# Two kinds of attention, four layers, one core: which score banks VectorE exponentiates is chosen while the program is written out, not beforehand

## The chip, the cores and the metric

One core of a Trainium2 chip. The time is that of one execution on the device, in microseconds (us); three executions of the kernel before took 2189.13, 2195.17 and 2195.78, median 2195.17. Engines: PE (TensorE, matrix products), ACT (ScalarE, here the exponentials), DVE (VectorE), POOL (GpSimd) and SP, which starts most loads. Each works through its own list of instructions in order and waits for the others by semaphores.

## What is computed

Four residual layers over x of 2048 rows and 640 columns, bf16: layers 0 and 2 with attention in a window of 256 keys (weights A), layers 1 and 3 with full attention over all 2048 keys (weights B). 32 heads of 20 columns.

```python
def _B_ref(x, wqkv, wo):
    ...
    scores = jnp.einsum("bhqd,bhkd->bhqk", q, k) * (Dh ** -0.5)
    p = _softmax(scores, axis=-1)
    o = jnp.einsum("bhqk,bhkd->bhqd", p, v)
    return (lambda x, *d: x.transpose(*d))(o, 0, 2, 1, 3).reshape(B, S, D) @ wo
...
x = A_x
x = x + _A_ref(_layernorm(x, axis=-1), A_wqkv, A_wo)
x = x + _B_ref(_layernorm(x, axis=-1), B_wqkv, B_wo)
x = x + _A_ref(_layernorm(x, axis=-1), A_wqkv, A_wo)
x = x + _B_ref(_layernorm(x, axis=-1), B_wqkv, B_wo)
```

`_A_ref` is the same with scores masked to keys at most 255 rows back.

## The kernel before

**Units, banks, tiles.** Queries go in four chunks of 512 rows, heads in eight groups of four. A *unit* (l, c, g) is the attention of layer l, query chunk c, head group g. Chunk 0 of layers 1 and 3 is cut by keys too: (3,0,g,(0,12)) does key blocks 0 to 11 of 16, (3,0,g,(12,16)) the last four, which only become known when chunk 3 of layer 2 is done. A *bank* is one head's scores of 128 keys against 512 queries: one PSUM bank, [128, 512]. A unit of full attention has 64 banks. The list `units` (L750 to L766) fixes the order: layer 0 mixed with the first part of layer 1, then layer 1 with the windowed units of layer 2 between, then layer 3. The "second layer" is layer 1, the "final layer" layer 3.

The main loop (L1324) writes out one *tile* at a time, mostly three banks: score matmuls into one of two halves of PSUM (banks 0 to 2, or 3 to 5), one exponential on ACT over all of it (L1387), and two or three tiles later the products with the values into bank 7 (`op`, L1420). Where a tile has the first bank of a unit not yet met, `state["unit"]` is set to that unit and `start_unit` is called (L1338 to L1348). The order of PE's instructions is the order in which the loop and the functions it calls write them.

**Background.** All other work is in generators (`Task`): `t_ln` (normalise and transpose a chunk), `t_v` (values, eight blocks of a chunk), `t_block` (keys or queries, five blocks of 128 columns), `t_out` (output projection and residual), `t_tail` (division by the softmax sums). Keys, queries and values go through DRAM (`k_d`, `q_d`, `v_d`): stored by POOL, loaded for a unit by `load_unit` on SP. `background` calls `pump` once a tile with a credit from `rate`, which looks how much is left to do until the unit that needs it (`starts`, in tiles), and then `keep_clock`, which adds matmuls that nobody reads (`unread`, or `owed` ones in the next tile) until the tile has 1.76 groups of background matmuls. Every step takes a PSUM bank by `take_m`. Once the wide units begin (`end_early`), bank 6 alone is left for this. A tail goes ahead of all other tasks. `load_ahead` loads the next units as soon as all that they need is `ready`; if a unit starts and something is not ready, `start_unit` calls `require`, which writes out the missing tasks on the spot.

**Banks for DVE.** Some banks are exponentiated by DVE instead: `side_fixed` reads the scores into fixed point (L957), `t_chain` makes the exponential of a pair of banks in four operations (L969, L978, L980, L982), `side_values` multiplies with the values. Before, `put_aside` names them when the units are made: the last banks of each unit, four in layer 1 (`SIDE_1`), six or eight in layer 3 (`SIDE_3`), none in chunk 0 and in (3,1,0). In layer 1 the list `tiles` is laid out in advance, with such a bank as the third of every fifth tile, its scores in the tile's own half of PSUM. In layer 3, chunks 1 to 3, one is started (`side_scores`, into bank 6, which it keeps for two ticks) when `state["lag"]`, an estimate of DVE's backlog, is under `LAG`. The buffers for it in layer 3 are three tiles of the pool of transposed chunks (`side_start`); this waits until no transposed chunk is alive and nothing is left to do.

Of the kernel before, what the change touches and what calls it, by code (L numbers as in the profile page):

```python
# [23 lines left out]
NT = S // P  # L24
# [15 lines left out]
LAG = 0.5  # L40
WORK = 1.0
SIDE_1 = 4
SIDE_3 = (6, 8)
# [9 lines left out]
def kernel(  # L53
# [272 lines left out]
    def evac(out_, in_):  # L326
        if state["act"]:
            nc.scalar.copy(out=out_, in_=in_)
        else:
            state["lag"] += 0.6  # L330
            nc.vector.tensor_copy(out=out_, in_=in_)  # L331
# [60 lines left out]
    def stats(l, c, i):  # L392
        if (l, c) not in mvs:
            mvs[l, c] = lnp.tile([P, 4, 2], F32, name="mv", tag="mv")
        state["lag"] += 1.2
        st = lnp.tile([P, 2, 6], F32, name="stats", tag="stats")
        xv = x_sb[:, 4 * c + i, :]
        nc.vector.bn_stats(out=st[:, 0, :], in_=xv[:, 0:HD])
        nc.vector.bn_stats(out=st[:, 1, :], in_=xv[:, HD:D])
        nc.vector.bn_aggr(out=mvs[l, c][:, i, :], in_=st[:])  # L400
# [282 lines left out]
    def put_aside(l, c, g):  # L683

        if l == 1:
            n = SIDE_1
        else:
            n = 4 if (c, g) == (NC - 1, G - 1) else SIDE_3[g % 2]
        if n == 2:
            return ((NT - 1, 2), (NT - 1, 3))  # L690
        return tuple((NT - 1 - i // 4, i % 4) for i in range(n))

# [3 lines left out]
    class Unit:  # L696
        def __init__(self, l, c, g, part=None):
            self.l, self.c, self.g, self.part = l, c, g, part
            self.windowed = l % 2 == 0
            self.aside = ()  # L700
            if self.windowed:
                sets = [(m, b0, subs, j) for m, b0, subs in window_banks(c) for j in range(4)]
            else:

                if c > 0 and (l, c, g) != (3, 1, 0):
                    self.aside = put_aside(l, c, g)
                k0, k1 = key_blocks(l, part)
                sets = [
                    (None, 0, [(kc, 0, 4, 0)], j) for kc in range(k0, k1) for j in range(4)
                    if (kc, j) not in self.aside  # L710
                ]
            n = len(sets)
            self.banks = [
                (self, j, m, b0, subs, i < 4, i >= n - 4 + len(self.aside), i == n - 1)
                for i, (m, b0, subs, j) in enumerate(sets)
            ]
# [144 lines left out]
    def finish_unit(u):  # L861
# [31 lines left out]
    side_todo = deque(  # L893
        (u, p, i) for u in units for p in range(len(u.aside) // 2) for i in range(2)
    )
    side_left = Counter({id(u): len(u.aside) for u in units})
    side_out = {}
    side = {"xi": deque(), "chain": deque(), "out": deque(), "late": False}
# [7 lines left out]
    def side_start():  # L906

        assert live["xnT"] == 0 and not side["chain"] 
        tl = [xtp.tile([P, KD, C], BF16, name="xnT", tag="xnT") for _ in range(3)]
        live["xnT"] += 3  # L910
        f = [v[:, 0:4, :].rearrange("p a b -> p (a b)").bitcast(F32) for v in tl]
        side["xi"].clear()
        side["out"].clear()
        outs = [ka_all[:, KA - 6 + 2 * n : KA - 4 + 2 * n, :] for n in range(3)]
        outs += [qa_all[:, 2 * n : 2 * n + 2, :] for n in range(2)]
        side_tiles(f[0:2], f[2].bitcast(F16)[:, 0 : 2 * C], outs)
        side["late"] = True
# [9 lines left out]
    def side_free():  # L927

        if not side_todo or not side["late"]:
            return False  # L930
        u, p, i = side_todo[0]
        return (
            id(u) in loaded and state["tick"] >= loaded[id(u)] + 8
            and mfree[6][0] <= state["tick"] and (i == 1 or len(side["xi"]) > 0)
        )

    def side_scores():

        u, p, i = side_todo[0]
        mseq[0] += 1  # L940
        mfree[6] = (state["tick"] + 2, mseq[0])
        kc, j = u.aside[2 * p + i]
# [4 lines left out]
    def side_fixed(z):  # L947

        u, p, i = side_todo.popleft()
        side_left[id(u)] -= 1  # L950
        if not side_left[id(u)] and id(u) in deferred:
            live["kt"] -= 1
            live["qt"] -= 1
        if i == 0:
            side["now"] = side["xi"].popleft()
        xi = side["now"]
# [33 lines left out]
    def side_work(force):  # L990

        while (force or state["lag"] < WORK) and side["chain"]:
# [11 lines left out]
    def side_values(u, pairs, done):  # L1004

        for n in range(done, len(pairs)):
            pt = pairs[n][0]
            for i in range(2):
                kc, j = u.aside[2 * n + i]
                nc.tensor.matmul(  # L1010
                    op[32 * j : 32 * j + VW, :], lhsT=u.v(kc, j), rhs=pt[:, i, :], start=False,
                    stop=all(jj != j for _, jj in u.aside[2 * n + i + 1 :]),
                    skip_group_check=True,
                )
            side["out"].append(pt)

    def side_push():
# [3 lines left out]
        if side_free():  # L1021
            side_scores()
# [7 lines left out]
    def side_done(u):  # L1030

        n = 0
        while len(side_out.get(id(u), ())) < len(u.aside) // 2:
            n += 1
            assert n < 10000
            side_push()
        return side_out.pop(id(u))
# [5 lines left out]

    def s_emitted(u):
# [6 lines left out]
        elif side_left[id(u)]:  # L1051
# [187 lines left out]
    with tc.manual_schedule():  # L1239
# [11 lines left out]
        banks = [b for u in units for b in u.banks]  # L1251
        tiles = []
        starts = {}
        n = 0
        last_layer = sum(len(u.banks) for u in units[: index[3, 1, 0, None]])
        placed = {}
        while n < last_layer:
            size = 2 if len(tiles) % 2 and narrow(banks[n][0]) else 3
            u = banks[n][0]
            at = placed.setdefault(id(u), [])  # L1260
            extra = []
            if (
                len(at) < len(u.aside) and banks[n + 1][0] is u
                and len(tiles) >= (15 // (SIDE_1 - 1) if SIDE_1 > 2 else 3) * len(at) + (at or [0])[0]
            ):
                kc, j = u.aside[len(at)]
                extra = [(u, j, "side", 0, [(kc, 0, 4, 0)], False, False, False)]
                at.append(len(tiles))
                size = 2
            for b in banks[n : n + size]:  # L1270
                starts.setdefault(id(b[0]), len(tiles))
            tiles.append(banks[n : n + size] + extra)
            n += size
        for m, b in enumerate(banks[n:]):
            starts.setdefault(id(b[0]), len(tiles) + m // 3)
        banks = deque(banks[n:])

        side_now = False

        def next_tile(t):  # L1280

            if t < len(tiles):
                return tiles[t]
            size = 3
            if side_now:
                return [banks.popleft() for _ in range(min(size, len(banks)))]
            if t % 2 and not tails and state["held"] is None and mfree[6][0] < state["tick"]:
                if all(task.wake > state["tick"] for task in todo) :
                    size = 4
            return [banks.popleft() for _ in range(min(size, len(banks)))]  # L1290

        def rate(t):

            if t >= len(tiles):
                return 0.45
            u = tiles[t][0][0]
            if index[u.l, u.c, u.g, u.part] < woven:
                return 1.2
            done, r = 0.0, 0.6 if state["early"] else 0.3
            for task in todo:  # L1300
                done += max(task.left, 0.0)
                if task.need < len(units):
                    r = max(r, done / max(starts[id(units[task.need])] - t - 16, 1))
# [10 lines left out]
        last_tick[0] = len(tiles)  # L1314
# [4 lines left out]
        valued = 0  # L1319
# [4 lines left out]
        while ended is None or t < ended + 8:  # L1324
# [3 lines left out]
            if t < len(tiles) or banks:  # L1328
                if t >= len(tiles) and not side["late"] and not live["xnT"] and not todo:
                    side_start()  # L1330
                side_now = (
                    state["held"] is None and state["lag"] < LAG and side_free()
                )
                cur = next_tile(t)
# [28 lines left out]
                if cur[-1][2] == "side":  # L1363
                    cur = cur[:-1]
                    n_b -= 1
                    if "early" not in side:
                        side_early()
                    while not side_todo[0][2] and not side["xi"]:
                        assert side_work(True)
                    side_fixed(sp[:, n_b, :])  # L1370
                if side_now:
                    side_scores()
# [28 lines left out]
            for n in range(2 if n_b == 0 or t > closed + 1 else 0):  # L1401
# [15 lines left out]
                for m, (kc, q0, qn, col) in enumerate(subs):  # L1417
                    for _, pg, i, b in group:
# [4 lines left out]
                            start=(first and m == 0), stop=(last and m == len(subs) - 1),  # L1423
                            skip_group_check=u.windowed or len(u.aside) > 0,
                        )
                if first:
                    valued = 0
                if u.aside and not end:
                    pairs = side_out.get(id(u), ())
                    if len(pairs) > valued and pairs[valued][1] + 3 <= state["tick"]:  # L1430
                        if valued + 1 < len(u.aside) // 2:
                            side_values(u, pairs[: valued + 1], valued)
                            valued += 1
                if end and u.aside:
                    side_values(u, side_done(u), valued)
# [87 lines left out]
```

## Time and profile before

| | us |
|---|---|
| median of three executions | 2195.17 (2189.13 to 2195.78) |
| the profiled execution | 2197.81 |
| its span, first to last instruction | 2196.1 |
| mean granted clock of PE in it | 0.993 |

Where the span goes, from the starts of the exponentials in the timeline (the first tile of each stretch):

| stretch | from | to |
|---|---|---|
| layer 0, and with it the first parts of layer 1's chunk 0 | 16.4 | 441.2 |
| last part of layer 1's chunk 0 | 441.2 | 498.6 |
| layer 1, chunks 1 to 3, with layer 2, chunks 0 to 2 | 498.6 | 1285.6 |
| layer 3, chunk 0, key blocks 0 to 11, with layer 2, chunk 3 | 1285.6 | 1501.5 |
| layer 3, chunk 0, key blocks 12 to 15 | 1501.5 | 1559.8 |
| layer 3, chunks 1 to 3 | 1559.8 | 2183.5 |

How to read it: a row of a group is line, engine, operation, output and input with their shapes, count; then busy time and mean duration in ns; then the engine's idle time just before these instructions and who ended it. A row of the timeline is start, duration, engine, line, operation. Matmuls into four strips of 32 columns run side by side, four instructions make one *group* (L307, L1420).

### The profile page before, as it was taken

Reading aid. Unit: us, or ns where it says so; the run is one execution under the profiler, and the core shown is the slowest. Engines: PE = TensorE matmul, PEld = TensorE weight load, DVE = VectorE, ACT = ScalarE, POOL = GpSimd, SP = SyncE. Lnnn points to the kernel's source line nnn. Section 1 sums busy time; section 2 is a strip of 40 time slices with the busy share of each in tenths; the row PEclk is TensorE's granted clock in tenths of the full one; section 3 lists DMA queues with packets and bytes.
Section 4 is the critical chain, followed back from the end, with each engine's and each line's share of the span. In section 5 each row is a group of like instructions: output and inputs, shape, how many; then the busy total and the mean of one; then the engine's idle time right before and its main releaser. Section 6 shows DMA issues by size and latency. Waiting matters only on the chain. (4 is left out here: it accounts for less than half of the span.)

```text
span 2196.1 us, 73000 instructions
## 1 busy us (share of the span) xinstructions
PE 1931.1 (88%) x31782; PEld 760.4 (35%) x31783; DVE 1324.3 (60%) x2308; ACT 2112.9 (96%) x1726; POOL 483.3 (22%) x952
## 2 busy tenths in 40 slices
PE   8999998988889888888888988888888988888887
PEld 3444443433333333333333433342222222222222
DVE  5556565425656666566665743532487778778873
ACT  7789899999999999999999999999999999999997
POOL 6665556110121113401143112511000000000000
PEclk9899999999999999999999999999999999999999
DMA  6223233322210323112231123122112111111100
GB/s 201 74 82 107 68 98 99 81 78 64 74 46 27 83 60 90 39 37 64 64 101 34 35 86 98 39 57 65 48 43 61 32 32 41 35 32 35 53 20 17
DMA packets 88416, 137.27 MB, mean 63 GB/s; under 512 B 20766, under 2 KB 63486, under 8 KB 88094
## 3 DMA queue, kind: packets, MB, share of 16 engines
q1 hardware_dynamic: 68878, 79.43, 13.1%
q0 software_dynamic: 19216, 53.17, 8.2%
q8 instruction: 249, 4.08, 0.8%
q14 instruction: 73, 0.60, 0.1%
HBM read 99.52 MB, written 27.79 MB: 58 GB/s over the span
## 5 line engine op out<-in xcount | busy, mean ns | idle before, releaser
L1387 ACT ACTIVATE pt<-ps 128x1536 bf16<-128x1536 f32 (+2 forms) x1646 | 2072.1, 1438 | 46.1 <-PE ps L1359 36.1
L1359 PE MATMUL ps<-qt,kt 32*128 32x512 bf16 x3938 | 542.4, 384 | 79.3 <-ACT pt L1387 70.2
L307 PE MATMUL ps<-masks,ident 128*32 128x512 bf16 x5676 | 504.6, 387 | 99.4 <-ACT pt L1387 54.8
L1420 PE MATMUL ps<-pt,vt 128*21 128x512 bf16 x3826 | 383.1, 387 | 1.1 <-issue 1.1
L1359 PEld LDWEIGHTS <-kt 32*128 32x128 bf16 x3938 | 161.0, 91 | 482.7 <-issue 461.0
L307 PEld LDWEIGHTS <-ident 128*32 128x32 bf16 x5676 | 179.9, 94 | 283.1 <-issue 254.7
L1463 POOL TENSOR_SCALAR_AFFINE_SELECT pt<-pt 128x256 bf16<-128x256 bf16 (+2 forms) x505 | 213.2, 444 | 184.4 <-ACT pt L1387 181.8
L307 PE MATMUL ps<-xnT,wqk 128*32 128x512 bf16 x3320 | 224.8, 381 | 12.4 <-DVE on L1128 2.8
L331 DVE CAST st<-ps 128x512 bf16<-128x512 f32 x134 | 92.7, 691 | 169.1 <-PE ps L307 164.9
L1420 PEld LDWEIGHTS <-vt 128*21 128x21 bf16 x3842 | 95.0, 89 | 254.9 <-issue 251.5
L957 DVE TENSOR_SCALAR xnT<-ps 128x512 int32<-128x512 f32 x158 | 109.2, 691 | 109.2 <-PE ps L944 108.4
L307 PE MATMUL ps<-wop,on 128*32 128x320 bf16 x3712 | 160.9, 300 | 6.8 <-DVE x_sb L579 3.3
L1474 DVE TENSOR_TENSOR pt<-pt,masks 128x512 bf16<-128x512 bf16 (+4 forms) x267 | 111.3, 433 | 61.3 <-ACT pt L1387 59.8
L307 PEld LDWEIGHTS <-on 128*32 128x32 bf16 x5760 | 122.2, 95 | 66.6 <-issue 33.6
L1359 PE MATMUL ps<-qa,ka 32*128 32x384 bf16 (+2 forms) x1408 | 114.5, 278 | 24.4 <-ACT pt L1387 21.2
L307 PE MATMUL ps<-wv,xnT 128*32 128x320 bf16 x2560 | 116.6, 302 | 7.9 <-DVE on L1128 3.3
L579 DVE TENSOR_TENSOR x_sb<-x_sb,ps 128x320 bf16<-128x320 bf16 x120 | 58.3, 486 | 105.8 <-PE ps L307 104.9
L307 PEld LDWEIGHTS <-wqk 128*32 128x32 bf16 x3320 | 83.5, 96 | 95.9 <-issue 38.0
L1128 DVE TENSOR_TENSOR on<-on,ps 128x512 bf16<-128x512 bf16 x128 | 86.3, 683 | 47.8 <-PE ps L307 46.9
L885 DVE CAST on<-ps 128x512 bf16<-128x512 f32 x112 | 77.1, 688 | 61.7 <-PE ps L1010 36.1
L957 DVE TENSOR_SCALAR raw_o<-ps 128x512 int32<-128x512 f32 x96 | 66.1, 689 | 61.4 <-PE ps L1359 60.3
L546 POOL DMA_DIRECT2D k_d<-st x75 | 42.6, 568 | 224.2 <-DVE st L331 209.1
(101 smaller groups left out, 1638.5 us busy)
## 6 DMA issues: line engine op xcount, KB each, us to landing
vt<-v_d SPq DMA_DIRECT2D x48, 336.0 KB
kt<-k_d SPq DMA_DIRECT2D x192, 80.0 KB
wqk<-in_B_wqkv_dram POOLq DMA_DIRECT2D x80, 160.0 KB, 3.5
wqk<-in_A_wqkv_dram POOLq DMA_DIRECT2D x70, 160.0 KB, 3.5
k_d<-st POOLq DMA_DIRECT2D x75, 128.0 KB, 2.3
q_d<-st POOLq DMA_DIRECT2D x75, 128.0 KB, 2.1
qt<-q_d SPq DMA_DIRECT2D x384, 20.0 KB
v_d<-vs POOLq DMA_DIRECT2D x16, 336.0 KB, 3.1
```

The source lines that it names most:

```text
L307: nc.tensor.matmul(out_[r], lhsT=lhsT[:, r], rhs=rhs, start=start, stop=stop)
L331: nc.vector.tensor_copy(out=out_, in_=in_)
L546: nc.gpsimd.dma_start(out=dst, in_=staging.pop())
L579: nc.vector.tensor_tensor(out=xv, in0=had, in1=yp, op=ALU.add)
L885: nc.vector.tensor_copy(out=oT, in_=op)
L957: nc.vector.tensor_scalar(out=xi.bitcast(I32)[:, i * C : (i + 1) * C], in0=z, scalar1=SCALE * LOG2E * FIX, scalar2=127.5 * FIX, op0=ALU.mu ...
L1128: nc.vector.tensor_tensor(out=oT, in0=oT, in1=zb, op=ALU.mult)
L1359: nc.tensor.matmul(sp[:, i, col * P : (col + qn) * P], lhsT=u.k(kc, j), rhs=u.q(j, q0, qn), start=True, stop=True,)
L1387: nc.scalar.activation(out=pt[:, i:k, b0 * P :], in_=sp[:, i:k, b0 * P :], func=ACT.Exp, scale=SCALE,)
L1420: nc.tensor.matmul(op[32 * j : 32 * j + VW, q0 * P : (q0 + qn) * P], lhsT=u.v(kc, j), rhs=pg[:, i, col * P : (col + qn) * P], start=(first ...
L1463: nc.gpsimd.affine_select(out=v, in_=v, compare_op=ALU.is_gt if later else ALU.is_ge, fill=0.0, base=0, pattern=[[0, k - i], [-1 if later ...
L1474: nc.vector.tensor_tensor(out=pt_[:, i:k, cols], in0=pt_[:, i:k, cols], in1=mv_, op=ALU.mult)
```

## The change

Every unit now has a queue `rest` from which the loop takes its next banks one by one (`pop`), instead of a list made in advance; `put_aside` and the list `tiles` are gone. Before each tile the loop asks `side_giver` for a unit that can give a bank to DVE: only while the lag is under `LAG` (`LAG_1` before layer 3's buffers are there), from the current unit or one of the next two that has been loaded for eight ticks, as long as it has 30 banks left (`KEEP`; 12 once it has begun to give); in layer 1 at most four a unit (`MOST_1`), in layer 3 without a limit. `side_take` takes two from the queue's end. Layer 1's chunk 0 is left out, layer 3's chunk 0 is not: `side_start` now comes from unit (3,0,4) on, as soon as at most one transposed chunk is alive. `rate` reckons the position from `state["unit"]` and what is left in it. Some estimates of lag change.

```diff
+LAG_1 = 0.5
 WORK = 1.0
-SIDE_1 = 4
-SIDE_3 = (6, 8)
+WORK_1 = 1.0
+KEEP = 30
+MOST_1 = 4
 QA = 4
...
-            state["lag"] += 0.6
+            state["lag"] += 0.7 if in_.shape[-1] == C else 0.5
...
-                if c > 0 and (l, c, g) != (3, 1, 0):
-                    self.aside = put_aside(l, c, g)
-                k0, k1 = key_blocks(l, part)
...
+                self.k0, k1 = key_blocks(l, part)
+                self.rest = deque((kc, j) for kc in range(self.k0, k1) for j in range(4))
+            self.size = len(self.rest)
+
+        def pop(self):
+
+            if self.windowed:
+                return self.rest.popleft()
+            kc, j = self.rest.popleft()
+            end = not self.rest
+            return (self, j, None, 0, [(kc, 0, 4, 0)], kc == self.k0, end, end)
 
...
-        assert live["xnT"] == 0 and not side["chain"] 
+        assert live["xnT"] <= 2 and not side["chain"] and side["half"] is None
...
+    def side_giver():
+
+        if side["half"] is not None:
+            return side["half"][0]
+        if not side["xi"]:
+            return None
+        while side["at"] < len(givers) and not givers[side["at"]].rest:
+            side["at"] += 1
+        for n in range(side["at"], min(side["at"] + 3, len(givers))):
+            u = givers[n]
+            if id(u) not in loaded or state["tick"] < loaded[id(u)] + 8:
+                return None
+            if not side["late" if u.l == 3 else "early"]:
+                return None
+            if u.l == 1 and len(u.aside) >= MOST_1:
+                continue
+            if len(u.rest) >= (KEEP if len(u.rest) + len(u.aside) < u.size else 12):
+                side["at"] = n
+                return u
+        return None
+
+    def side_take(u):
+
+        if side["half"] is not None:
+            return side["half"][1]
+        j = u.rest.pop()
+        i = u.rest.pop()
+        u.aside += (i, j)
+        side["half"] = (u, i, j)
+        return i
...
+        starts, spans = {}, {}
+        n = 0.0
+        for u in units:
+            starts[id(u)] = n
+            spans[id(u)] = u.size / (2.5 if narrow(u) else 3.0)
+            n += spans[id(u)]
+        flow = deque(units)
...
+        def next_tile(t, giver):
+
+            if state["unit"] < final:
+                size = 2 if t % 2 and narrow(flow[0]) else 3
+                if giver is None or giver.l == 3 or size == 2:
+                    return take(size)
+                kc, j = side_take(giver)
+                return take(2) + [(giver, j, "side", 0, [(kc, 0, 4, 0)], False, False, False)]
...
-            if index[u.l, u.c, u.g, u.part] < woven:
+            u = units[state["unit"]]
+            if state["unit"] < woven:
                 return 1.2
+            now = starts[id(u)] + spans[id(u)] * (1 - len(u.rest) / u.size)
             done, r = 0.0, 0.6 if state["early"] else 0.3
             for task in todo:
                 done += max(task.left, 0.0)
                 if task.need < len(units):
-                    r = max(r, done / max(starts[id(units[task.need])] - t - 16, 1))
...
+                if not side["early"] and state["unit"] >= index[1, 1, 0, None]:
+                    side_early()
+                if (
+                    not side["late"] and state["unit"] >= index[3, 0, 4, PARTS[3][0]]
+                    and live["xnT"] <= 1 and not live["qa"] and not live["ka"]
+                ):
                     side_start()
-                side_now = (
-                    state["held"] is None and state["lag"] < LAG and side_free()
-                )
-                cur = next_tile(t)
+                if state["unit"] >= final:
+                    last_tick[0] = 0
+                giver = side_giver() if state["lag"] < (LAG if side["late"] else LAG_1) else None
+                if giver is not None and giver.l == 3 and (
+                    state["held"] is not None or mfree[6][0] > state["tick"]
+                ):
```

## The prediction

> **What bounds the kernel now.** First the shares of busy time, then ACT's groups by shape.
>
> ```profile
> PE 1931.1 (88%) x31782; PEld 760.4 (35%) x31783; DVE 1324.3 (60%) x2308; ACT 2112.9 (96%) x1726; POOL 483.3 (22%) x952
> ...
> L1387 ACT ACTIVATE pt<-ps 128x1536 bf16<-128x1536 f32 x1321 | 1816.3, 1549 | 37.0 <-PE ps L1359 28.4 <-POOL pt L1463 3.0 <-issue 1.7
> L1387 ACT ACTIVATE pt<-ps 128x1024 bf16<-128x1024 f32 x245 | 261.2, 1070 | 8.4 <-PE ps L1359 7.8
> L1387 ACT ACTIVATE pt<-ps 128x512 bf16<-128x512 f32 x21 | 13.3, 639 | 0.0
> ```
>
> ACT is nearly always busy, and with exponentials. Their ends overlap, so the price of a tile is read from starts, in the chain of waits:
>
> ```profile
> 1530.56 0.64 ACT pt L1387
> 1531.89 0.65 ACT pt L1387
> 1533.22 0.67 ACT pt L1387
> ```
>
> 1.33 us per 1536-column tile. From the starts of all exponentials in the timeline, 1024 columns take 0.90, 768 0.69, 512 0.48, 256 0.26. With these widths, all waiting of ACT from the start of unit (1,1,0) at 498.6 us to the end adds up to 47 us; 92 us lie before (layer 0 and its mixture with layer 1), where the change alters nothing but a few fillers. So behind 498 us a bank that leaves ACT is worth its full width, and whatever delays the next scores by more than about one tile is paid in full: the PSUM halves let PE be one tile ahead, no more.
>
> PE has little room. A tile's scores and its value matmuls begin 0.33 us apart each (timeline at 1440.75, 1441.07, 1441.41), a four-strip group of 512 columns adds 0.21 and one of 320 columns 0.13; `keep_clock` fills up to 1.76 groups a tile. A tile with eight groups of 320 needs 0.66 + 1.17 = 1.83 us, more than 1.33.
>
> **The change, part by part.** *Banks taken from ACT.* The instruction orders of both programs give the counts: layer 1 hands 96 banks to DVE in both (24 units, four each, so the cap of four changes nothing in number), layer 3 hands over 186 instead of 158. ACT's instructions go 1321 to 1316 (1536 columns), 245 to 238 (1024), 28 to 26 (768), 21 to 26 (512), 15 to 13 (256): 5 x 1.33 + 7 x 0.90 + 2 x 0.69 - 5 x 0.48 + 2 x 0.26 = 12.5 us less (14.7 by mean durations). Of the 28 banks 22 come from layer 3's chunk 0: ten pairs from units (3,0,4) to (3,0,7) and one from (3,0,4,(12,16)). The DVE work for them (14 chains of 0.69, 0.69, 1.22 and 1.22 us and 28 reads of 0.69, together 73 us) lies beside ACT, DVE being 60% busy. Cost of their reads on bank 6 by the row of units (3,1,0) to (3,1,7), which do the same now: 7.3 us of waiting in eight units against 0.8 in (3,0,4) to (3,0,7); four units: +2 (0 to 4).
>
> *What this moves.* Bank 6 is the only PSUM bank for background work by then, and each score on it blocks it for two ticks, each tail, `out` or projection step having to find it free. In the order of before, the last tail of layer 2 ends early in (3,0,4), `out(2,3)` follows, `ln(3,3)` and the values fill (3,0,5) and (3,0,6), and keys block 0 stands 17 tiles ahead of (3,0,0,(12,16)), the first unit that needs them. In the changed order the tails of layer 2 crawl through (3,0,4) and (3,0,5), `out(2,3)` gets one 320-column step of eight groups every fifth tile, its last four in consecutive tiles (4 x 0.5 over, less the one tile of lead: +1.5), and nothing of `ln(3,3)` but its rstd stands before the first tile of (3,0,0,(12,16)). There `start_unit` calls `require`, and on PE, ahead of that tile's scores, stand in one piece: four transposed rows of `ln(3,3)`, all eight value blocks, keys block 0; on SP behind it the loads of `vt`, `qt`, `kt`. The whole runs through bank 6 alone, PE and DVE in turn. The same pieces now, from the timeline:
>
> ```profile
> 1457.17 0.46 PE L447 MATMUL ps<-ident,xn 128*32 128x128 bf16 x20
> 1457.69 0.49 DVE L331 COPY xnT<-ps 128x640 bf16<-128x640 bf16 x1 [0.43 <-PE ps L447]
> 1461.09 0.86 PE L307 MATMUL ps<-wv,xnT 128*32 128x320 bf16 x20 [0.18 <-DVE xnT L331]
> 1462.00 0.49 DVE L331 CAST vs<-ps 128x320 bf16<-128x320 f32 x1 [0.96 <-PE ps L307]
> 1462.55 0.86 PE L307 MATMUL ps<-wv,xnT 128*32 128x320 bf16 x20
> 1479.87 1.25 PE L307 MATMUL ps<-xnT,wqk 128*32 128x512 bf16 x20
> 1481.18 0.69 DVE L331 CAST st<-ps 128x512 bf16<-128x512 f32 x1 [3.55 <-PE ps L307]
> ```
>
> A value block takes 1.46 us from start to start (0.91 until its eviction, 0.49, 0.06), eight 11.7. A transposed row takes 0.21 of fillers, 0.52 and 0.49 + 0.06: 1.28; four with the first without fillers 4.9. Keys 1.25 + 0.05 + 0.69 = 2.0. Then the round trip through DRAM:
>
> ```profile
> 1476.93 0.69 DVE L331 CAST st<-ps 128x512 bf16<-128x512 f32 x1 [2.54 <-PE ps L307]
> 1477.93 0.56 POOL L546 DMA_DIRECT2D k_d<-st  x1 [0.50 <-DVE st L331]
> 1480.72 0.28 SPq L812 DMA_DIRECT2D kt<-k_d  x1
> 1482.17 0.33 SPq L812 DMA_DIRECT2D kt<-k_d  x1
> 1556.50 2.03 DMA kt<-k_d
> ```
>
> Eviction done at 1477.62, first `kt` issue at 1480.72, the third strip, which the tile's third bank reads, 1.45 later, landed 2.03 later: 6.6 us. With 0.4 for scores and about 1.1 until the first normalised row is there (0.16 + 0.47 behind a 1.22 chain step), the chain is 1.1 + 4.9 + 11.7 + 2.0 + 6.6 + 0.4 = 26.7 us, counted from where these scores would have been issued; ACT has one tile left: 25.4 us of standstill. No other unit may run meanwhile, since ACT and PE go in order.
>
> PE's clock makes it longer:
>
> ```profile
> 50.10:53.50 3.40, 1.22 (x37) 1.00 0.74 190
> 53.00:56.00 3.00, 2.83 (x54) 1.46 (x58) 0.74 (x2) 1.78 (x3) 0.78 (x2) 0.59 0.32 82
> 1517.80:1521.25 3.45, 2.25 (x57) 1.00 0.34 99
> 1521.25:1524.70 3.45, 3.45 (x32) 0.51 0.06 17
> ```
>
> (PE's busy time, then the granted clock.) After 3.4 us with 2.25 us busy or less the clock was granted at half for 3.4 us. In the value chain PE is busy 0.86 of 1.46, 59%, in the rows of transposes less; at half clock a value block's PE part grows by about 0.65. Half of the blocks cold: 4 x 0.65, with rows and keys about +3.5 (0 to 7). I take 29 us for the standstill, 22 to 35.
>
> The Trainium skill, "TensorE: Matmul & The Clock Gate", Part 1, has the clock halve after an idle window of some 3.4 us. The trace's 2.25 of 3.45 us is not idle and was followed by half clock all the same. By the page's wording the 3.5 us would be nothing and the standstill 25.4; I go by the row.
>
> *Next late:* keys block 1, for (3,0,1,(12,16)), is put out behind the second tile after the standstill: 0.74 for the fourth strip, two 0.33 for values, 0.2 for the side values, 1.25 to 2.3 on PE (clock cold after 6.6 us of idling), 0.75, 3.1 to the first `kt`, 0.74 and 2.03 to the second strip, 0.4: 10 to 11 us, with five tiles, 6.7 us, to cover it: +4 (2 to 6). The remaining key and query blocks have unloaded PE then and are hidden by that wait.
>
> *Layer 1.* The banks go as lag allows, also from units one or two ahead, and that marks such a unit as started: `state["unit"]` jumps ahead and then stays there while earlier units still run, so `rate` is first high, later low. Projection groups per tile: 2.5 or more in 8 of 24 units before (1.5 us of waiting each in the trace; the other 16 have 0.8 each), in 13 units in the changed order, six of them at 3.0 to 3.3; the fillers of layers 1 and 2 grow by 71 groups where the work is missing. 5 x 0.7 = 3.4 at least by the class means, 9 if those above 3 wait twice that: +5 (-2 to 10, since the spread within a class is as large as the step).
>
> Sum: -12.5 + 2 + 1.5 + 29 + 4 + 5 = +29. The profiled execution took 2197.8 (span 2196.1 and 1.7 around it), so 2226.8; it lies 2.6 above the median of 2195.2, so 2224 for a median.
>
> **Rivals.** *The chain is shorter.* PE alone would need 8 x 0.86 + 4 x 0.45 + 1.25 = 9.9 us; if evictions hid and the clock held, with 7.0 for the round trip and 1.1 at the front, 18 - 1.3 = 16.7: sum +14 with layer 1 at +3, 2209. For it: DVE is idle then. Against: one bank, and 1462.55 follows 1462.49. Chance 0.15.
>
> *Everything is cold.* Half clock through all the chain and on through the blocks behind it, standstill 35, layer 1 +10, next wait 6: +42, 2237. For it: the busy shares above; against: at half clock PE is busy over 65%, which gives the clock back. Chance 0.2.
>
> *The gain stands: faster.* The chain's place is in the order, so only its length can save it: it decides once the standstill and what follows stay below 12.5 - 2. With 3 us left of it and layer 1 at its better bound, -12.5 + 2 + 3 - 2 = -9.5: 2186. That needs PE to run the whole chain under the exponentials of earlier tiles. Against: PE goes in order, has one tile of lead, and the landing of `kt` alone takes 2.03 us. Chance 0.05.
>
> *No change.* The shares cancel: standstill 16.7, nothing behind it, layer 1 -2: +3, 2198. Chance 0.04. That the change does not do what it says can be excluded: the banks are counted.
>
> **Numbers.** Forecast 2224, chance 0.56; with the rivals above 0.15, 0.2, 0.05, 0.04. The range takes the bounds of the standstill (-7, +6) and of layer 1 (-7, +5) and reaches to both slower rivals: 2206 to 2244. About 0.3% (6.6 us) is what a measurement can tell here: faster 0.05, same 0.04, slower 0.91.
>
> **What would show it.** After: one gap of ACT of 25 to 33 us at some 1500 us, released by PE L1381 or the `kt` DMA, with the eight `wv` blocks in it 1.4 to 2.2 us apart; a second gap of 2 to 6 us about 7 us later; half clock in between; ACT about 14 us less busy, DVE 73 more; waits for PE in layer 1 up by about 5. The prediction is wrong if the largest gap there is under 15 us, or if layer 1 moves by more than 10.

## The result and the profile after

| | before | after |
|---|---|---|
| median of all runs, us | 2192.98 (2189.13 to 2195.78, 4 runs) | 2248.21 (2243.69 to 2250.67, 4 runs) |
| ratio | | 1.0251, 95% interval 1.0225 to 1.0276: slower |
| profiled execution, us (span) | 2197.81 (2196.1) | 2250.67 (2248.4) |

The change costs 55 us where +29, a median of 2224, had been forecast; the time lies outside the range of 2206 to 2244. The page of the changed kernel, its busy shares, ACT's and the clock's rows over 40 slices of 56 us, and the group of exponentials (busy time, mean ns of one, idle time of ACT ahead of it):

```profile
PE 1966.1 (87%) x32178; PEld 766.6 (34%) x32179; DVE 1391.4 (62%) x2394; ACT 2105.8 (94%) x1715; POOL 487.5 (22%) x954
...
ACT  7899899998999999999999989993999999999998
...
PEclk9999999999999999999999999996999999999999
...
L1405 ACT ACTIVATE pt<-ps 128x1536 bf16<-128x1536 f32 (+2 forms) x1635 | 2065.2, 1419 | 111.0 <-PE ps L1381 99.5
```

The same group on the page of the kernel before:

```profile
L1387 ACT ACTIVATE pt<-ps 128x1536 bf16<-128x1536 f32 (+2 forms) x1646 | 2072.1, 1438 | 46.1 <-PE ps L1359 36.1
```

ACT has less to do and is idle more: 111.0 us ahead of exponentials, 46.1 before. One slice, the 28th, shows a 3 for ACT and a 6 for the clock: that is a standstill. The other slices hide the rest of it. So all waits were taken stage by stage, from the starts of all exponentials less the widths given in the prediction (1.33, 0.90, 0.69, 0.48 and 0.26 us). A wait stands with the unit whose tile comes before it:

| ACT's waiting, us | before | after |
|---|---|---|
| up to 498 us (layer 0 and its mixture) | 91.5 | 89.4 |
| layer 1, chunks 1 / 2 / 3 | 5.9 / 8.1 / 11.2 | 16.5 / 14.1 / 20.7 |
| layer 2 in between | 3.6 | 4.2 |
| (3,0,g,(0,12)) | 2.9 | 43.0 |
| (2,3,g) and (3,0,g,(12,16)) | 0.2 + 1.1 | 0.9 + 4.7 |
| (3,1), (3,2), (3,3) | 7.3 + 3.6 + 3.6 | 6.1 + 3.4 + 3.1 |
| all | 139.0 | 206.1 |

+67.1 of waiting and 12.5 less of exponentials (2029.0 to 2016.5 by these widths) make +54.6; the spans differ by 52.3. The growth in layer 1 shows in the profile's own list of waits too (total, times, longest), from 499 to 1285 us, first before, then after:

```profile
ACT pt L1387 <- PE ps L1359: 11.0, 28, 0.9
```

```profile
ACT pt L1405 <- PE ps L1381: 25.6, 50, 1.1
```

There are two large single gaps: 33.9 us by starts, in the row (3,0,g,(0,12)) of the table, and 7.9 us, in chunk 3 of layer 1. The first is the forecast one, here in the timeline of the changed kernel (start, length, engine, operation; in brackets the idle time before and what ended it):

```profile
1519.82 2.79 ACT L1405 ACTIVATE pt<-ps 128x1536 bf16<-128x1536 f32 x2 [1.08 <-PE ps L1381]
...
1524.39 0.46 PE L449 MATMUL ps<-ident,xn 128*32 128x128 bf16 x20 [2.93 <-DVE xn L429]
...
1530.68 1.52 PE L309 MATMUL ps<-wv,xnT 128*32 128x320 bf16 x20 [0.59 <-DVE xnT L333]
...
1532.25 0.49 DVE L333 CAST vs<-ps 128x320 bf16<-128x320 f32 x1 [1.62 <-PE ps L309]
1532.80 1.52 PE L309 MATMUL ps<-wv,xnT 128*32 128x320 bf16 x20 [0.60 <-DVE vs L333]
...
1547.63 1.97 PE L309 MATMUL ps<-xnT,wqk 128*32 128x512 bf16 x20 [0.59 <-DVE vs L333]
...
1550.63 0.56 POOL L548 DMA_DIRECT2D k_d<-st  x1 [1.76 <-DVE st L333]
...
1552.69 0.28 SPq L808 DMA_DIRECT2D kt<-k_d  x1
...
1554.40 1.87 PE L1381 MATMUL ps<-qt,kt 32*128 32x512 bf16 x3 [4.80 <-DMA kt<-k_d]
...
1556.36 2.79 ACT L1405 ACTIVATE pt<-ps 128x1536 bf16<-128x1536 f32 x2 [33.75 <-PE ps L1381]
```

The rows of `ln(3,3)`, eight value blocks, keys block 0, its store, its load, and then the scores: 33.75 us without an exponential. A value block takes 2.12 us from start to start (1530.68, 1532.80). The second gap had not been forecast. It stands in the chain of waits of the changed kernel (start, length, what the end waited for):

```profile
1299.24 0.75 POOL v_d L506
...
1301.04 2.97 DMA k_d<-st
...
1305.47 2.15 DMA kt<-k_d
```

That is the first tile of (3,0,0,(0,12)): the instruction order shows that the last key block it needs, block 0 of chunk 2, is written out, with the last of the values, in the very tile whose scores read it; in the kernel before, the unit's loads start 15 tiles ahead. Its trip through DRAM (2.97 and 2.15 us) lies bare: 7.9 us.

### The profile page after: what moved, and what is told of

It is laid out like the page before. It is cut to its first block, busy times and chain, and to the rows that moved or that the text cites. A ratio compares the mean times of both kernels' runs of the same rounds, so it can differ in the third digit from the quotient of the medians.

```text
span 2248.4 us, 73798 instructions
## 1 busy us (share of the span) xinstructions
PE 1966.1 (87%) x32178; PEld 766.6 (34%) x32179; DVE 1391.4 (62%) x2394; ACT 2105.8 (94%) x1715; POOL 487.5 (22%) x954
## 3 DMA queue, kind: packets, MB, share of 16 engines
q1 hardware_dynamic: 68878, 79.43, 13.4%
## 4 chain that ended last, share of the span: by engine, by line
ACT 43%; PE 28%; issue 14%; DVE 12%; DMA 1%; POOL 1%; SPq 0%; ACTq 0%; DVEq 0%; POOLq 0%
ACT pt L1405 42%; PE ps L309 16%; PE ps L1381 7%; PE ps L1438 3%; DVE on L1151 2%; DVE st L333 1%; DVE raw_o L999 1%; DVE ka L999 1%; DVE raw_o L976 1%; DVE x_sb L581 1%; PE ps L449 1%; DVE xnT L976 1%; DVE pt L1487 1%; PE ps L960 1%; DVE xnT L988 1%
## 5 line engine op out<-in xcount | busy, mean ns | idle before, releaser
L1405 ACT ACTIVATE pt<-ps 128x1536 bf16<-128x1536 f32 (+2 forms) x1635 | 2065.2, 1419 | 111.0 <-PE ps L1381 99.5
L309 PE MATMUL ps<-masks,ident 128*32 128x512 bf16 x6072 | 530.7, 387 | 99.1 <-ACT pt L1405 60.3
L1381 PEld LDWEIGHTS <-kt 32*128 32x128 bf16 x3910 | 154.6, 91 | 492.9 <-issue 460.5
L1476 POOL TENSOR_SCALAR_AFFINE_SELECT pt<-pt 128x128 bf16<-128x128 bf16 (+2 forms) x507 | 216.9, 449 | 252.6 <-ACT pt L1405 213.1
L976 DVE TENSOR_SCALAR xnT<-ps 128x512 int32<-128x512 f32 x186 | 128.5, 691 | 130.4 <-PE ps L960 129.2
L415 POOL TENSOR_SCALAR rstd<-mv 128x4 f32<-128x4 f32 x15 | 5.4, 363 | 405.8 <-DVE mv L402 405.5
L548 POOL DMA_DIRECT2D k_d<-st x75 | 42.8, 570 | 206.1 <-DVE st L333 185.7
```

What stands on the lines that cost most here:

```text
L309: nc.tensor.matmul(out_[r], lhsT=lhsT[:, r], rhs=rhs, start=start, stop=stop)
L976: nc.vector.tensor_scalar(out=xi.bitcast(I32)[:, i * C : (i + 1) * C], in0=z, scalar1=SCALE * LOG2E * FIX, scalar2=127.5 * FIX, op0=ALU.mu ...
L1381: nc.tensor.matmul(sp[:, i, col * P : (col + qn) * P], lhsT=u.k(kc, j), rhs=u.q(j, q0, qn), start=True, stop=True,)
L1405: nc.scalar.activation(out=pt[:, i:k, b0 * P :], in_=sp[:, i:k, b0 * P :], func=ACT.Exp, scale=SCALE,)
L1476: nc.gpsimd.affine_select(out=v, in_=v, compare_op=ALU.is_gt if later else ALU.is_ge, fill=0.0, base=0, pattern=[[0, k - i], [-1 if later ...
```

## The experiments

The times of e5_ownhalf, e8_most6, e9_bgfirst_timed and e10_spread are medians of 6 to 12 executions, the others those of one execution; single executions of the kernel before lie between 2187 and 2200. "Waits" are ACT's waits behind 498 us as in the table above (47.5 before, 116.7 after); the part ahead of it, which no edit touches, came out between 83.9 and 91.5 us.

The theory after the result had two parts, "A" in the expectations of e1_flow to e6_bgfirst: the standstill comes from bank 6, which scores of chunk 0 keep from the background; and layer 1 loses because a side bank sets `state["unit"]`, from which `rate` takes the time that is left. In the changed order that variable jumps up to two units ahead and at the end of layer 1 stays at (2,2,7) for 65 tiles, in which the background gets about a third of a group of credit a tile.

**e1_flow: a side bank no longer sets the unit.**

```diff
                 for b in cur:
                     u = b[0]
                     if id(u) not in started:
+                        if b[2] == "side":
+                            continue
                         started.add(id(u))
```

> The changed kernel, but a bank given to VectorE ahead of its turn no longer marks its unit as started, so the background's rate reads the unit that really runs. Theory A (the waits of layer 1 and the gap before (3,0,0,(0,12)) come from the rate): ACT's waiting between 498 us and (3,0,0,(0,12)) falls from about 57 to about 28 us, the 34 us standstill at (3,0,0,(12,16)) stays: about 2220 us. Rival B (the waits of layer 1 come from the side banks themselves, bunched and read late from PSUM): only the gap of 8 to 10 us before (3,0,0,(0,12)) goes: about 2238.

Measured: 2227.58, 23 less than after. Layer 1 waits 12.1 / 8.7 / 7.6, 28.4 in place of 51.3; the gap of 7.9 is gone; the standstill is there unchanged, 33.8 us. The time is 7.6 above the forecast value; most of it is that the first units of chunk 1 keep their waits: the jump of the variable was not all of layer 1's loss, but 22.9 of its 26.1 us.

**e2_nochunk0: chunk 0 of the final layer gives no banks.**

```diff
-    givers = [u for u in units if not u.windowed and (u.l, u.c) != (1, 0)]
+    givers = [u for u in units if not u.windowed and u.c > 0]
```

> The changed kernel with chunk 0 of layer 3 left out of the giving; its three early buffers are still taken from unit (3,0,4) on. Theory A (side banks on PSUM bank 6 starve the background there): the 34 us standstill and the 4 us behind it go, 20 banks come back to ACT (9 us): about 2217. Rival C (the early buffers keep the normalisation of chunk 3 from starting): the standstill stays, about 2255.

Measured: 2217.78, 33 less than after. The units (3,0) wait 4.5 us in place of 47.7; layer 1 (16.4 / 14.1 / 20.8) and the gap of 7.9 us stay. Where the answer on ACT's waits from 1400 to 1600 us of the changed kernel reads

```profile
ACT pt L1405 <- PE ps L1381: 40.8, 11, 33.7
```

(total, times, longest), the same stretch of e2_nochunk0, to 1580 us, shows no wait for scores. The time is theory A's; that of the rival, early buffers, would have been 38 us longer, and it falls.

**e3_both: both edits.**

> Both of these edits: giving tile by tile from the backlog as in the changed kernel, rate by the running unit, chunk 0 of layer 3 left out. Theory A: no long gap is left, exponentials 3.6 us less than before: about 2190. Rival B: waits of layer 1 stay 18 us above before's: about 2208.

Measured: 2196.48 (span 2194.7), waits 48.9. The two edits alone save 23.1 and 32.9 us, together 54.2: the two losses add up, and together they are the whole of what the change costs, to within the few us by which single executions differ. It is 6 us over the expected time. Chunk 1 (10.7) and layer 2 (7.8) keep waits that the kernel before doesn't have, though others are shorter and all waits together only 1.4 longer; from the start of the last exponential to the end it takes 15.6 us in place of 12.7, which was not explained. Whether bank 6 or VectorE's work itself makes the standstill is not told apart by it, as both go with chunk 0's banks; e5_ownhalf does that.

**e4_distort: the kernel before with only the rate distorted.** Its `rate` reads, in tiles 349 to 957, the positions that the changed kernel's variable had there (a list of 51 unit changes); banks and their places stay as before.

```diff
...
+            now = t
+            if t in SEEN:
+                seen[0] = index[SEEN[t]]
+            if seen[0] is not None and t < 958 and u is not units[seen[0]]:
+                here = index[u.l, u.c, u.g, u.part]
+                now = starts[id(units[seen[0] + (seen[0] < here)])]
...
-                    r = max(r, done / max(starts[id(units[task.need])] - t - 16, 1))
+                    r = max(r, done / max(starts[id(units[task.need])] - now - 16, 1))
```

> The kernel before, its banks untouched, but from tile 349 to 957 the rate takes the position that the changed kernel's state gave at the same tile (a list of the tiles at which it moved). Theory A: waits of layer 1 rise from 28 to about 55 us, with a gap of 8 to 10 before (3,0,0,(0,12)): about 2220. Rival B: only that gap: about 2203.

Measured: 2213.32 (span 2211.5, 15 more than before). Layer 1 waits 12.6 / 11.0 / 17.6, with a gap of 6.8 us ahead of (3,0,0,(0,12)), and (3,0,g,(0,12)) 7.1. So the rate by itself makes 16 of layer 1's 26 us, the gap included, in a kernel that has nothing else of the change. The expected 2220 was too high: the rest is not the rate alone.

**e5_ownhalf: chunk 0 gives banks, but not through bank 6.** Each takes the third bank of its tile's own half, as in layer 1; e1_flow's edit is in it too. A sentence of the theory was at stake here: that banks of chunk 0 cost nothing once bank 6 is left alone.

```diff
-                if giver is None or giver.l == 3 or size == 2:
+                if giver is None or size == 2:
...
-                if giver is not None and giver.l == 3 and (
+                if giver is not None and giver.l == 3 and state["unit"] >= final and (
```

> The changed kernel with the two repairs that the theory asks for. A side bank no longer sets the current unit, and chunk 0 of the final layer still gives banks to VectorE, but each takes the third bank of the tile's own PSUM half, so that bank 6 stays with the projections and layer norms. Theory A (the standstill comes from bank 6 being taken, not from the banks of chunk 0 being worked by VectorE): the chain at the end of unit (3,0,7) runs as in the kernel before, no gap over 5 us on ScalarE from tile 350 on, waits in all 135 to 142 as in e3_both, exponentials' widths 2014 (11 less than e3_both): profiled 2185 (2181 to 2190), a ratio to the kernel before of about 0.994. Rival C (VectorE's extra work for chunk 0 delays value and key blocks whatever bank it uses): a gap of 10 us or more is back before (3,0,0,(12,16)), 2195 to 2220.

Measured: 2199.75, ratio to before 1.003 (1.0018 to 1.0041). No standstill, no unit forced, but also no gain: waits 66.4, of them 13.4 in (3,0,g,(0,12)) and 6.0 in (3,0,g,(12,16)), against 1.5 and 0.8 in e3_both. That is 17 us for exponentials 11 us narrower. The window from 1420 to 1520 us, first of e3_both, then of e5_ownhalf (length, then the busy times of PE, PEld, DVE, ACT, POOL, granted clock, DMA share, GB/s):

```profile
1420.00:1520.00 100.00, 86.08 (x1375) 34.82 (x1373) 29.23 (x60) 100.00 (x76) 16.59 (x25) 1.00 0.23 62
```

```profile
1420.00:1520.00 100.00, 85.08 (x1240) 31.64 (x1228) 76.05 (x114) 85.87 (x69) 16.23 (x24) 0.93 0.22 58
```

DVE goes from 29 to 76 us busy, and ACT from 100 to 86. What PE waited for there in e5_ownhalf (total, times, longest):

```profile
PE ps L309 <- DVE st L333: 3.2, 5, 1.5
PE ps L1031 <- DVE ka L1001: 2.6, 1, 2.6
PE ps L309 <- DVE x_sb L581: 2.0, 4, 0.9
PE ps L309 <- DVE vs L333: 1.7, 3, 0.8
```

Background matmuls go through one bank, which DVE has to empty; with exponentials of 1.22 us a step ahead of it in DVE's list, that comes late, and PE's queue with the next scores stands behind. The 2.6 are side values whose pair was not done when its unit ended. In e3_both PE's longest waits in the same stage are for ACT. So the standstill is bank 6's doing, but the rival named in the expectation is right in a smaller form: not one gap of 10 us, but 17 us in all, the largest gap 3.4. That DVE's work in chunk 0 costs this is shown; how much of it is DVE's lateness is not. PE's clock was at half from 1451.3 to 1458.1 and from 1512.7 to 1519.6 us (0.93 in the row above), and 7.9 us of ACT's waits lie in these two stretches; and a tile that hands its third bank to DVE gives PE the cover of 1024 columns, 0.90 us, in place of 1.33.

**e6_bgfirst and e9_bgfirst_timed: chunk 0 gives a bank only where no background is left.** With e1_flow's edit; four banks of chunk 0 in place of 22.

```diff
                     state["held"] is not None or mfree[6][0] > state["tick"]
+                    or (state["unit"] < final and side["half"] is None and (tails or todo))
                 ):
                     giver = None
```

> The changed kernel with the flow repair, and chunk 0 of the final layer gives banks (through bank 6, as in the change) only in tiles in which no background work is left to do. Theory A: VectorE gets almost none of chunk 0's banks (4 in place of 22), the standstill is gone, exponentials' widths 2024, waits about 139: 2195 (2191 to 2200). A rule that keeps bank 6 for the background leaves nothing of chunk 0 for VectorE, so it is worth about 10 us less than e5_ownhalf. Rival C: the same time as e5_ownhalf or better.

> e6_bgfirst once more, timed in rounds beside the kernel before, as the base for e10_spread. Exponentials 4.6 us narrower than in the kernel before, waits 2 us longer: a ratio of 0.998 (0.996 to 1.0005). So what is left of the change, VectorE's one bank in 58 of chunks 1 to 3 of the final layer and the new way of forming tiles, is worth at most 0.3%.

Measured: 2193.18 in one execution, 2191.5 as a median of twelve, ratio 0.9996 (0.9986 to 1.0007), waits 52.0 and 50.8. Better than e5_ownhalf by 0.34% going by the ratios, some 7 us, the opposite of what the sentence on 10 us had said: here the theory's idea of free capacity in chunk 0 fell. With both faults mended the change is worth nothing that can be measured.

**e7_most2 and e8_most6: two or six side banks a unit in layer 1** (`MOST_1`, on e5_ownhalf).

> e5_ownhalf with two side banks a unit in layer 1 in place of four. Theory B1 (the rest of the excess in layer 1's chunk 1, some 4 us in units (1,1,0) to (1,1,2), comes from VectorE's exponentials bunched at the start of a unit's work): chunk 1 back to 6 to 8 us of waits, exponentials 20.5 us wider than in e5_ownhalf, 2201 (2197 to 2205). Theory B2 (it comes from the rate of the background alone, whose tiles come the same): chunk 1 stays at 10 to 12, 2205 (2203 to 2209).

> e5_ownhalf with six side banks a unit in layer 1. VectorE is busy 62% of the span in the changed kernel; 48 more banks at about 0.9 us are 43 us of some 2190, two points more. Exponentials 20.4 us narrower than in e5_ownhalf. Theory B1 (bunching costs waits): chunk 1 to 3 wait 4 to 5 us more each, 2177 (2171 to 2182). Theory B2 (the rate alone): waits as in e5_ownhalf, 2165 (2161 to 2170). If VectorE or TensorE becomes the bound in layer 1, no faster than e5_ownhalf.

Measured: 2214.50 with two (one execution), 2199.75 with four, 2199.48 with six (ratio to before 1.0031, 1.0022 to 1.0041). The waits of layer 1's chunks are 6.4 / 4.3 / 6.7 with two, 11.7 / 7.5 / 7.7 with four, 15.2 / 17.8 / 19.6 with six. Both absolute times lie above what was expected, in part because e5_ownhalf did; the differences decide. From two to four, exponentials save 20.5 us and waits give back 9.5; from four to six they save 20.4 and lose 25.7 there. So waits do grow with side banks while the rule for the rate stays (B1). But from four to six they grow by 3.5, 10.3 and 11.9 us a chunk, where B1 had 4 to 5, and the 8 us forecast between e5_ownhalf and e8_most6 are missing: the third case of the expectation, no faster than e5_ownhalf, came true. The cap of four stands where a further bank brings nothing. From 499 to 777 us DVE is busy 227 of the 278 us with six and 182 in e5_ownhalf with four, PE 250 and 244; which of the two sets the limit is not shown.

**e10_spread: pairs in layer 1 at least ten tiles apart** (on e6_bgfirst). By DVE's reads in the traces, most pairs of the kernel before come 9 to 12 tiles apart there, the first of e6_bgfirst 3 to 9.

```diff
+            if u.l == 1 and state["tick"] < side["last"] + 10:
+                return None
...
+        side["last"] = state["tick"]
```

> e6_bgfirst with one condition more: in layer 1 a pair of side banks starts at least ten tiles after the last one, as the pairs of the kernel before did (they come 10 to 14 tiles apart there, 6 or 7 apart in the first units of e6_bgfirst, and up to three units ahead of their turn). The number of side banks and the widths stay. Theory D (in layer 1 what remains after the flow repair comes from crowded pairs): waits of chunk 1 fall from 12 us to 6 to 8, those of the layer from 27 to 20 to 24, 3 to 6 us faster than e9_bgfirst_timed, ratio 0.995 to 0.997. Theory B2 (it comes from the rate, which is set by positions that run three banks a tile while side tiles carry two): chunk 1 stays at 10 to 13, same time as e9_bgfirst_timed within 2 us.

Measured: 2189.62, ratio to before 0.999 (0.9979 to 1.0001), against 2191.5 of e9_bgfirst_timed. Chunk 1 waits 7.6 in place of 11.4 and the layer 22.6 in place of 27.6, as theory D had it; but layer 2 and (3,1) wait 1.7 and 2.6 more, which takes most of it back, and the intervals of the two kernels overlap: the waits are theory D's, the time is not its 0.995 to 0.997. So crowding is a cause of chunk 1's excess (its 3.8 us are well over the 0.8 by which the same program differed in two traces), and removing it gained no more than the 2 us that were seen.

**e11_fillchain: two groups of unread matmuls after every step of the forced chain** (on the changed kernel): after its value and key blocks, and in the trace after the rows of `ln(3,3)` too, which are written out on the same call.

```diff
-            state["credit"] = max(state["credit"] - advance(t), -1.0)
+            n_pe = advance(t)
+            state["credit"] = max(state["credit"] - n_pe, -1.0)
+            if n_pe and state["held"] is None and what[0] in "vk" and what[1:3] == (3, 3):
+                for _ in range(2):
+                    by_columns(ps[:, state["next"], :], ident, masks[:, 0, :], True, True)
...
+            state["next"] = 3 * (t % 2)
```

> The changed kernel with 2 x 4 matmuls that nobody reads after every value and key block of the forced chain, so that TensorE is not idle while VectorE empties a block. Nothing else moves. Theory (the chain's excess over the forecast is the half clock in all of its blocks, where half of them were taken as cold): the granted clock in the chain comes back to 1.0 after the first 3 to 7 us, a value block takes 1.4 to 1.6 us in place of 2.12, and the standstill falls from 33.9 to 27 to 30 us: 2244 to 2247 profiled. Rival (the length of the chain is set by VectorE's and the queues' steps, and the clock only shows the idle time): block to block stays at 2.1 and the standstill within 1.5 us of 33.9, or grows by the matmuls added.

Measured: 2242.62, 8 less than after; the standstill is 27.8 us by starts, 6.1 less. Its timeline, two value blocks with the filling between them:

```profile
1531.74 0.86 PE L313 MATMUL ps<-wv,xnT 128*32 128x320 bf16 x20 [0.16 <-DVE vs L337]
1532.42 0.62 PE L313 MATMUL ps<-masks,ident 128*32 128x512 bf16 x8
...
1533.20 0.86 PE L313 MATMUL ps<-wv,xnT 128*32 128x320 bf16 x20 [0.16 <-DVE vs L337]
...
1548.86 1.45 ACT L1410 ACTIVATE pt<-ps 128x1536 bf16<-128x1536 f32 x1 [27.66 <-PE ps L1386]
```

0.86 instead of 1.52 us for the same 20 matmuls, 1.46 from block to block. More work for PE made the chain shorter, so the clock was part of its length and not only a sign of idling.

## Why the prediction was wrong, point by point

*The step that failed* is the term for layer 1, "+5 (-2 to 10)". It measured +26.1 (25.2 to 51.3 us), 7.9 of it the second gap. The mechanism was named rightly, `state["unit"]` that jumps ahead and then stays, and e1_flow and e4_distort show it at work; what was mis-sized is its price. It was worked out from classes of units by groups per tile, 0.7 us for each unit that changes class. Three things lie outside of that:

- The low rate has an end of its own: after 65 tiles at a third of a group a key block was missing, and a second load was forced, 7.9 us. The lead of every load over the first tile that needs it stood in the order beforehand; the prediction gives it only for the units of the large standstill. The prediction's own mark, "if layer 1 moves by more than 10", caught it.
- In the first units of each chunk the waits grow not by 0.7 but by 2 to 6 us a unit: (1,1,1) goes from 0.6 to 6.2, (1,2,1) from 0.4 to 3.8, (1,3,1) from 0.9 to 3.4. In chunks 2 and 3 that is the rate, too high there: with e1_flow's edit these two units wait 0.9 and 1.1. In (1,1,1) 4.7 us stay with it, and 1.9 once the pairs are spread as well.
- Side pairs stand closer, which the prediction counted as no change because their number stays at 96. e10_spread puts this at some 4 us in chunk 1.

By e4_distort the rate alone makes 16 of the 26 us; in the changed kernel, where the pairs are crowded too, taking the jumps away gives back 22.9 (e1_flow). Crowding alone is worth about 4 to 5 (e10_spread). The 5 or 6 us between these figures may be the two together; that was not taken apart.

*The standstill*, "29 us", 22 to 35, measured 33.9, inside its bounds. The place, the eight blocks, the bank and the release by scores were as forecast. What was mis-sized in it is the clock, "half of the blocks cold", 3.5 us: all were, and e11_fillchain puts it at 6.1 or a little more, since its own chain starts with 3.4 us at half clock. The chain without the rest of the half clock is 27.8, where the rows had given 25.4. The rival "everything is cold" was right on this point with its 35; the reason given against it fell, "at half clock PE is busy over 65%, which gives the clock back". The window of the changed kernel from 1525 to 1549 us (PE 17.11 of 23.84 us busy, clock 0.50), the last 3.41 us of it, and two windows of e11_fillchain:

```profile
1525.24:1549.08 23.84, 17.11 (x248) 9.46 (x251) 6.29 (x14) 0.00 (x0) 1.77 (x3) 0.50 0.16 34
```

```profile
1545.69:1549.10 3.41, 2.82 (x36) 1.38 (x32) 0.49 (x1) 0.00 (x0) 1.53 (x2) 0.50 0.30 101
```

```profile
1523.30:1526.70 3.40, 3.40 (x72) 1.89 (x64) 1.69 (x4) 0.00 (x0) 0.76 (x2) 0.50 0.90 154
1526.70:1530.10 3.40, 3.07 (x84) 1.71 (x73) 1.35 (x3) 0.00 (x0) 0.00 (x0) 1.00 0.04 8
```

72% busy kept half clock for 24 us; the two windows of 3.41 us ahead of the last one have 2.53 and 2.23 us busy. In the changed kernel full clock came back behind the last one, which has the longer key block in it, 2.82 of 3.41 us busy; in e11_fillchain it came back behind a stretch of 3.4 us without a break.

*The exponentials*, -12.5: exactly that by widths. The page shows only 7.1 us less of ACT's busy time (2112.9 to 2105.8), not the 14 forecast as a mark, because ends overlap: two tiles in a row are 2.79 us of busy time, and the last one ahead of a wait counts 1.45 instead of 1.33. Starts are the better measure. *DVE*: +67 us busy, 73 forecast.

*Side reads and `out(2,3)`* ahead of the standstill, 2 + 1.5: 4.3 us, with 1.9 more just behind the missed gap. The 1.5 doesn't follow from its own rows: eight groups of 0.13 are 1.04, not 1.17, and four times 0.5 less a tile of 1.33 is 0.7. The rival "no change" adds up to about +6, not +3. *The next wait*, +4: +3.6, but the size is luck. It was forecast as one gap, the trip of keys block 1 through DRAM. The changed kernel has three, of 2.0, 1.3 and 0.7 us by starts, and PE waits for no load right before the scores that end them; these stand behind whole key or query blocks, the first two at half clock for most of their length (it lasts from 1552.5 to 1562.8 us). The first:

```profile
1558.02 2.35 PE L309 MATMUL ps<-xnT,wqk 128*32 128x512 bf16 x18
...
1561.02 1.45 ACT L1405 ACTIVATE pt<-ps 128x1536 bf16<-128x1536 f32 x1 [1.87 <-PE ps L1381]
```

The prediction counted the first such block only as a part of that trip, and had the others "hidden by that wait".

Stages that had been left out changed by -1.9 ((3,1) to (3,3)) and -2.1 (up to 498 us).

The sum with the measured terms is -12.5 + 6.2 + 33.9 + 3.6 + 26.1, with +1.3 for layer 2 and (2,3) and -4.0 for the stages left out: +54.6. Four fifths of the miss of 26 lie in layer 1, the rest in the clock and the length of the chain.

*A reason that was not in the prediction at all* came from e5_ownhalf: the DVE work of chunk 0, "beside ACT, DVE being 60% busy", is not free. In that stage DVE is busy only 29% in e3_both and 76% in e5_ownhalf, and by PE's waits its latency comes onto the path, since it empties the one bank of the background.

## What to carry to other kernels

Where an order is made by a planner, any variable that it steers by must not be written by work that runs ahead of its turn; after a change, compare for every unit the lead of its last load over its first use, not only for the unit that looks worst. An engine that is seldom busy can still be on the path if it empties the only buffer between two steps: its free time may be room for short work only, not for chains of long instructions. And before work is given to it, look whether the stage has waits to lose: here a stage with ACT at 100% lost 17 us for the 11 it was spared.

## What the runs showed of the hardware

TensorE's granted clock fell to half behind a stretch in which it was far from idle, 2.25 of 3.45 us busy (before). In the forced chain it stayed at half for 23.9 us with 72% busy and came back behind a window of 2.82 of 3.41 us (83%); in e11_fillchain 3.40 of 3.40 us ended it, and 89% busy (10.35 of the 11.65 us of the eight filled blocks) kept full clock. No fixed share for the way back follows from this: behind the second gap of the changed kernel, 1306.75 to 1310.16 us, 3.06 of 3.41 us busy (90%) at half clock were followed by another 3.4 us of it. In "TensorE: Matmul & The Clock Gate", Part 1, the Trainium skill has the half clock follow an idle window of some 3.4 us and the full clock a window of sustained work; the first does not agree with these runs, since 2.25 of 3.45 us were busy, the second does with the windows of 83% and 100%, while that of 90% did not suffice. For a chain in which two engines take turns, eight unread matmuls a step paid for themselves: 1.46 in place of 2.12 us a block, 6 us in all.
